# Gates and ups as pairs of 64-row half tiles, with one list of PSUM banks, in a fused attention and GeGLU kernel

## The chip, the cores and the metric

The kernel runs on one core of one Trainium2 chip. The time is device time of one execution in microseconds, the median of 3 runs: 220.92 us before (220.37 to 220.95). The profile is of one more execution, which took 221.15 us; its span, from the first to the last of the program's own instructions, is 219.4 us.

## The reference

For 2048 tokens of width 448: a layer norm, then attention over a sliding block of 256 tokens and a GeGLU feed-forward net, both on the normed x, and the sum of both with x.

```python
xn = _layernorm(x)                                     # 2048 x 448
qkv = xn @ wqkv                                        # 16 heads of 28
scores = (q @ k.T) * 28 ** -0.5                        # key within the last 256 tokens
o = softmax(scores) @ v
return x + o @ wo + (gelu(xn @ w_gate) * (xn @ w_up)) @ w_down   # F = 1792
```

## The kernel before, in words

The tokens are cut into four blocks of 512 (`qb`, 0 to 3), each of four tiles of 128. `xnT` holds the normed x transposed, 448 rows as three chunks of 128 and one of 64. The 64-row chunk stands twice, on partitions 0 to 63 and 64 to 127, so that two 64-row matmuls can use it at once, one on each half of the array's rows.

Each block has two parts. In `attention` a loop goes over steps (12 in block 0, 10 in the others): the step's score matmuls, an exponential of them on ScalarE (L622), and, at three steps, the product with the values of a group of four heads (`pv`, L576), which leaves two halves that ScalarE and VectorE add (`add_halves`). Between a step's scores and the next, TensorE is given other work from feeds: generators that issue a few matmuls and yield their cost. `gen_qk` and `gen_v` make keys, queries and values (in block 0 also those of block 1), `gen_down` makes the output of the block before (4 + 14 matmuls for each tile of tokens), and `gen_up` makes some ups early (in blocks 0 and 3), which a copy puts into `hT` (L415). A generator that yields HOLD is not run on within its step; it ends, with its 64-row matmuls, at the start of the next step. `share` and `plan` say how much of which feed goes into a step.

Then comes `gated`: for pairs of 128-wide tiles of F the gate and up products, a GELU of two tiles on ScalarE (L464), and the product of both into `hT` on VectorE (L471, or L469 for early ups). Each product is three matmuls of 128 rows (`three`, L232) and one of 64 (`half`, L238). Two 64-row matmuls on the two halves run side by side, and they are gathered: the dense matmuls of one pair, then the 64-row ones of two or three pairs, then the dense ones of the others. The last value product of the block (`last_v`) is issued behind the first 64-row ones, which in blocks 1 to 3 are cut into 32 columns, as the value product is.

The weights: `wg` and `wu` hold 384 rows of the gates and ups on 128 partitions, `wgu3` and `wug3` the last 64 rows of both, crosswise on the two halves. SyncE's queue issues nearly all loads in program order: x, the attention weights, the up weights (L144 to L146), x of tiles 8 to 11 (L147), a small part of the key weights (L174), later the DMA transposes of tiles 4 to 15 (L217), and in `loads` the gate weights and the rest. The x of tiles 0 to 3 is transposed on TensorE (`transp`).

PSUM has eight banks: four for scores or gates (`score_pool`), and four for the rest under three names: `m` (two of them), `d` and `o`. `bank` goes round a ring of names for projections and early ups, `gen_down` gets a string of names, `gated` alternates by `turn`. In blocks 1 to 3 a chunk of the output work is issued ahead of the first scores (`feeds[0].run()`).

```python
for fs in ((0, 2), (4, 8, 6), (10, 12)) if qb in (0, 3) else ((0,), (2, 4), (6, 8), (10, 12)):
    prs = [begin(fs[0])]
    dense(prs[0], True)
...
    for pr in prs:
        halves(pr, pr is not prs[0], 32 if qb and not fs[0] else P)
...
    for pr in prs[1:]:
        dense(pr, False)
        end(pr)
```

Of the kernel before, what the change touches and what calls it, by code (L numbers as in the profile page):

```python
# [75 lines left out]
def kernel(  # L76
# [38 lines left out]
    wg = const.tile([P, 3, F], bf16, name="wg")  # L115
    wu = const.tile([P, 3, F], bf16, name="wu")
    wgu3 = const.tile([P, F], bf16, name="wgu3")
    wug3 = const.tile([P, F], bf16, name="wug3")
# [3 lines left out]
    def rows(w, c0, n):  # L122
        return w[c0 * P:(c0 + n) * P, :].rearrange("(c p) n -> p c n", p=P)

# [19 lines left out]
    nc.sync.dma_start(out=wu[:, :, :], in_=rows(B_w_up, 0, 3))  # L144
    nc.sync.dma_start(out=wug3[0:64, :], in_=B_w_up[384:448, :])
    nc.sync.dma_start(out=wgu3[64:128, :], in_=B_w_up[384:448, :])  # L146
    nc.sync.dma_start(out=x_sb[:, 8:12, :], in_=xv[:, 8:12, :])  # L147
# [33 lines left out]
    xnT = const.tile([P, 4, S], bf16, name="xnT")  # L181
    qT = const.tile([P, 4, S], bf16, name="qT")
# [59 lines left out]
    ring = [("m", "m", "d"), 0]  # L242

    def bank(name):

        tag = ring[0][ring[1] % len(ring[0])]
        ring[1] += 1
        return psum.tile([P, QB], f32, name=name, tag=tag, bufs=2 if tag == "m" else 1)
# [8 lines left out]
    def v_copy(t, pv, copy):  # L257
        copy(out=v_sb[:, t, :, 0:Dh], in_=pv.rearrange("p (h d) -> p h d", d=Dh))

    def gen_v(qb, ts):  # L260

        for t in ts:
            pvs = []
            for i in range(2):
                pvs.append(bank("pv")[:, 0:D])
                v_dense(t + i, pvs[i])
                yield (570, HOLD) if i else 570
            for i in range(2):
                v_half(t + i, pvs[i])
            for i in range(2):  # L270
                v_copy(t + i, pvs[i], nc.vector.tensor_copy if qb > 1 or i else nc.scalar.copy)
            yield -360
# [10 lines left out]
    def qk_copies(qb, g, pq, pk):  # L283
        ts = slice(qb * QB, (qb + 1) * QB)
        nc.scalar.copy(out=qT[:, g, ts], in_=pq)
        nc.vector.tensor_copy(out=kT[:, g, ts], in_=pk)
        done.add((qb, g))

    def gen_qk(qb, gs, others=()):

        for g in gs:
            pq = bank("pq")[:, :]
            proj(pq, wqp, qb, g)
            if qb and g == 3:
# [4 lines left out]
                nc.scalar.copy(out=qT[:, 3, ts], in_=pq)  # L299
                done.add((qb, 3))  # L300
# [3 lines left out]
            pk = bank("pk")[:, :]  # L304
# [52 lines left out]
    UP1 = 1660  # L357
    STEP, PV = 450, 870

    hTs, oNs = {}, {}  # L360
    down_tag, last_tag, last_res = ["d"], [None], []

    def gen_down(qb, tags):

        hT, oN = hTs[qb], oNs[qb]
        for tt in range(4):
            t = 4 * qb + tt
            cs = slice(tt * P, (tt + 1) * P)
            for n, (lo, up) in enumerate(((0, D),) if t < NT - 1 else ((0, D // 2), (D // 2, D))):
                w = up - lo  # L370
                tag = tags[tt + n]
                down_tag[0] = tag
                po = psum.tile([P, QB], f32, name="po", tag=tag, bufs=2 if tag == "m" else 1)
# [11 lines left out]
                nc.vector.tensor_tensor(out=res[:, 0:w], in0=po[:, 0:w], in1=x_sb[:, t, lo:up], op=ALU.add)  # L385
                nc.sync.dma_start(out=outv[:, t, lo:up], in_=res[:, 0:w])
# [7 lines left out]
    def half(ps, f, gate, hi, ts, start, stop, m=P):  # L394

        w3 = wgu3 if gate != bool(hi) else wug3
        mm_half(ps, w3[:, f * P:(f + 1) * P], xnT[:, 3, ts], hi, start, stop, m)

    def three(ps, f, gate, ts, start, stop):
        w = wg if gate else wu  # L400
        mm3(ps, lambda c: w[:, c, f * P:(f + 1) * P], lambda c: xnT[:, c, ts], start, stop)

    def gen_up(qb, fs):

        ts = slice(qb * QB, (qb + 1) * QB)
        for f in fs:
            us = []
            for i in range(2):
                us.append(bank("ue"))
                three(us[i][:, :], f + i, False, ts, True, False)  # L410
                yield (650, HOLD) if i else 650
            for i in range(2):
                half(us[i][:, :], f + i, False, i, ts, False, True)
            for i in range(2):
                nc.vector.tensor_copy(out=hTs[qb][:, f + i, :], in_=us[i][:, :])  # L415
            yield -360

    def gated(qb, early, last_v, flush, hook):

        ts = slice(qb * QB, (qb + 1) * QB)  # L420
        hT = hTs[qb]
        turn = ["o" if down_tag[0] == "d" else "d", down_tag[0]] * 4

        def single(name, tag):
            return psum.tile([P, QB], f32, name=name, tag=tag, bufs=2 if tag == "m" else 1)[:, :]

        def begin(f, apart=False):
            last_tag[0] = turn[0] if f not in early else last_tag[0]
            pr = dict(f=f, us=[])
            if apart:  # L430
                pr["gs"] = [single("g0", tag) for tag in ("m", turn.pop(0))]
                return pr
            pr["gt"] = phase[0].pool.tile([P, 2, QB], f32, name="gt", tag="s")
            pr["gs"] = [pr["gt"][:, i, :] for i in range(2)]
            if f not in early:
                tags = ("m", turn.pop(0))
                if qb == 0 and f == 0:
                    tags = [ring[0][(ring[1] + i) % 3] for i in range(2)]
                    if "d" in tags:
                        turn.insert(0, "o")  # L440
                pr["us"] = [single("u0", tag) for tag in tags]
            return pr

        def dense(pr, start):
            f = pr["f"]
            gs = [(g, f + i, True) for i, g in enumerate(pr["gs"])]
            us = [(u, f + i, False) for i, u in enumerate(pr["us"])]
            for ps, fi, gate in (gs + us if f else us + gs):
                three(ps, fi, gate, ts, start, not start)

        def halves(pr, start, m):
            f = pr["f"]
            for i in range(2):
                if pr["us"]:
                    half(pr["gs"][i], f + i, True, 0, ts, start, not start, m)
                    half(pr["us"][i], f + i, False, 1, ts, start, not start, m)
                else:
                    half(pr["gs"][i], f + i, True, i, ts, start, not start, m)

        def end(pr):  # L460
            f = pr["f"]
            ge = work.tile([P, 2, QB], bf16, name="ge", bufs=2)
            if "gt" in pr:
                nc.scalar.activation(out=ge[:, :, :], in_=pr["gt"][:, :, :], func=ACT.Gelu_apprx_tanh)  # L464
            else:
                for i, g in enumerate(pr["gs"]):
                    nc.scalar.activation(out=ge[:, i, :], in_=g, func=ACT.Gelu_apprx_tanh)
            if not pr["us"]:
                nc.vector.tensor_tensor(out=hT[:, f:f + 2, :], in0=ge[:, :, :], in1=hT[:, f:f + 2, :], op=ALU.mult)  # L469
            for i, u in enumerate(pr["us"]):  # L470
                nc.vector.tensor_tensor(out=hT[:, f + i, :], in0=ge[:, i, :], in1=u, op=ALU.mult)  # L471
                flush()
# [478 lines left out]
```

## Time and profile before

| | |
|---|---|
| median of 3 runs | 220.92 us |
| the profiled execution, its span | 221.15 us, 219.4 us |
| first early up | 19.49 us |
| gated part of blocks 0, 1, 2, 3 begins | 37.76, 84.54, 136.03, 187.06 us |
| first scores of blocks 1, 2, 3 | 56.10, 107.58, 159.07 us |
| last output alone begins | 201.86 us |

In the views, PE is TensorE's matmuls and PEld its weight loads, DVE is VectorE, ACT ScalarE, POOL GpSimd, SP SyncE; a q behind the name is the engine's queue issuing a DMA. A timeline row gives start, length, engine, line, operation, what is written from what, the form (rows*columns of the array, then the moving operand) and how many instructions were merged. A row of the windows gives the window, its length, each engine's busy time and instructions, the granted TensorE clock, the DMA engines' share and GB/s.

### The profile page before, as it was taken

How to read it: one execution, taken by the hardware profiler on the slowest of the kernel's cores; microseconds unless marked ns; L12 is line 12 of the kernel's file. 1: busy time of each engine (PE TensorE's matmuls, PEld its weight loads, DVE VectorE, ACT ScalarE, POOL GpSimd, SP SyncE). 2: the span in 40 equal slices, each digit the busy share in tenths (PEclk: the TensorE clock that was granted, in tenths of full speed). 3: DMA queues.
4: the chain of work that ended last, by engine and by line, in shares of the span. 5: the costliest groups of instructions: out<-in, count | busy, mean ns of one | idle time of the engine just before them, and what ended most of it. 6: DMA issues, size and time to landing. Idle time of an engine off the chain costs nothing.

```text
span 219.4 us, 5447 instructions
## 1 busy us (share of the span) xinstructions
PE 213.9 (98%) x2287; PEld 96.1 (44%) x2287; DVE 152.1 (69%) x346; ACT 133.3 (61%) x131; POOL 46.9 (21%) x80
## 2 busy tenths in 40 slices
PE   7999999999999999999999999999999999999993
PEld 2433333434444454444444445444344445444562
DVE  6787896799666883679565795386356799479521
ACT  3588788662878875432878888233486777565000
POOL 5377987320000120022000022022000022022001
PEclk9999999999999999999999999999999999999998
DMA  6993799104200001102300000200000000000011
GB/s 193 310 311 71 188 325 302 30 4 72 45 3 21 24 24 27 20 3 46 60 13 24 23 1 24 52 13 0 0 3 21 25 3 24 24 1 0 22 35 37
DMA packets 18045, 13.30 MB, mean 61 GB/s; under 512 B 8704, under 2 KB 16992, under 8 KB 18016
## 3 DMA queue, kind: packets, MB, share of 16 engines
q1 hardware_dynamic: 17072, 12.62, 21.1%
q8 instruction: 19, 0.31, 0.6%
q10 hardware_dynamic: 944, 0.29, 0.5%
q14 instruction: 10, 0.08, 0.1%
HBM read 9.15 MB, written 2.18 MB: 52 GB/s over the span
## 4 chain that ended last, share of the span: by engine, by line
PE 96%; ACT 1%; DVE 1%; issue 1%; DVEq 0%
PE po L380 20%; PE gt L232 16%; PE u L232 12%; PE sc L616 6%; PE po L375 6%; PE gt L238 5%; PE ue L232 5%; PE ov L576 5%; PE pq L232 4%; PE pv L232 4%; PE pk L232 3%; PE wps L191 2%; PE pq L238 1%; PE g L232 1%; PE ue L238 1%; PE pv L238 1%
## 5 line engine op out<-in xcount | busy, mean ns | idle before, releaser
L622 ACT ACTIVATE p_sb<-sc 128x2048 bf16<-128x2048 f32 (+2 forms) x42 | 73.8, 1758 | 12.6 <-PE sc L616 8.2
L380 PE MATMUL po<-wd,hT 128*128 128x448 bf16 (+1 forms) x238 | 49.8, 342 | 0.0
L464 ACT ACTIVATE ge<-gt 128x1024 bf16<-128x1024 f32 x26 | 26.6, 1024 | 34.9 <-PE u L238 20.1
L542 POOL TENSOR_TENSOR oN<-oc,l 128x512 bf16<-128x512 f32 x12 | 16.0, 1334 | 137.8 <-DVE l L556 87.4
L232 PE MATMUL gt<-xnT,wg 128*128 128x512 bf16 x156 | 37.5, 380 | 0.0
L471 DVE TENSOR_TENSOR hT<-ge,u 128x512 bf16<-128x512 bf16 x40 | 25.7, 682 | 12.9 <-ACT ge L464 12.9
L380 PEld LDWEIGHTS <-hT 128*128 128x128 bf16 x238 | 21.5, 98 | 18.8 <-issue 2.6
L232 PE MATMUL u<-xnT,wu 128*128 128x512 bf16 x120 | 29.2, 379 | 0.0
L523 DVE TENSOR_TENSOR p_sb<-p_sb,masks 128x256 bf16<-128x256 bf16 (+1 forms) x90 | 26.8, 353 | 0.4 <-ACT p_sb L622 0.4
L232 PEld LDWEIGHTS <-wg 128*128 128x128 bf16 x168 | 15.3, 98 | 21.3 <-issue 4.5
L232 PEld LDWEIGHTS <-wu 128*128 128x128 bf16 x168 | 16.0, 98 | 19.2 <-issue 1.0
L561 DVE TENSOR_TENSOR oc<-oc,ov 128x512 f32<-128x512 f32 x12 | 8.2, 687 | 16.5 <-ACT oc L560 16.5
L616 PE MATMUL sc<-qT,kT 28*64 28x320 bf16 (+7 forms) x640 | 16.9, 263 | 0.2
L415 DVE CAST hT<-ue 128x512 bf16<-128x512 f32 x16 | 10.2, 681 | 8.4 <-PE ue L238 8.3
L375 PE MATMUL po<-wo,oN 128*128 128x448 bf16 (+1 forms) x68 | 15.9, 343 | 0.0
L385 DVE TENSOR_TENSOR res<-po,x_sb 128x448 bf16<-128x448 f32 (+1 forms) x17 | 10.0, 586 | 8.6 <-PE po L380 8.4
L533 POOL TENSOR_SCALAR_AFFINE_SELECT p_sb<-p_sb 128x512 bf16<-128x512 bf16 (+1 forms) x20 | 14.2, 730 | 5.0 <-ACT p_sb L622 4.8
L238 PE MATMUL gt<-xnT,wgu 64*128 64x512 bf16 (+1 forms) x67 | 12.7, 380 | 0.0
L560 ACT COPY oc<-ov 128x512 f32<-128x512 f32 x12 | 7.0, 583 | 8.8 <-PE ov L576 8.8
L232 PE MATMUL pq<-xnT,wqp 128*128 128x512 bf16 x45 | 12.2, 380 | 0.1
L548 DVE STREAM_TRANSPOSE l<-oc 128x512 f32<-128x512 f32 x16 | 11.3, 704 | 1.4 <-POOL oN L542 1.2
L232 PE MATMUL ue<-xnT,wu 128*128 128x512 bf16 x48 | 12.0, 380 | 0.0
(97 smaller groups left out, 241.9 us busy)
## 6 DMA issues: line engine op xcount, KB each, us to landing
out_dram<-res SPq DMA_DIRECT2D x15, 112.0 KB
x_sb<-in_A_x_dram SPq DMA_DIRECT2D x3, 448.0 KB
wu<-in_B_w_up_dram SPq DMA_DIRECT2D x1, 1344.0 KB
wg<-in_B_w_gate_dram SPq DMA_DIRECT2D x1, 1344.0 KB
wd<-in_B_w_down_dram SPq DMA_DIRECT2D x3, 448.0 KB
wraw<-in_A_wqkv_dram SPq DMA_DIRECT2D x2, 252.0 KB
wo<-in_A_wo_dram SPq DMA_DIRECT2D x4, 98.0 KB
wv<-in_A_wqkv_dram SPq DMA_DIRECT2D x1, 336.0 KB
```

The costliest lines, as they stand in the source:

```text
L232: nc.tensor.matmul(ps, lhsT=lhs(c), rhs=rhs(c), start=start and c == 0, stop=stop and c == 2, skip_group_check=True)
L238: nc.tensor.matmul(ps[c:c + m], lhsT=lhs[p0:p0 + 64, c:c + m], rhs=rhs[p0:p0 + 64], start=start, stop=stop, tile_position=(p0, c), skip_gr ...
L375: nc.tensor.matmul(po[:, 0:w], lhsT=oN[:, g, cs], rhs=wo[:, g, lo:up], start=(g == 0), stop=False, skip_group_check=True)
L380: nc.tensor.matmul(po[:, 0:w], lhsT=hT[:, f, cs], rhs=wd[:, f, lo:up], start=False, stop=(f == NF - 1), skip_group_check=True)
L464: nc.scalar.activation(out=ge[:, :, :], in_=pr["gt"][:, :, :], func=ACT.Gelu_apprx_tanh)
L471: nc.vector.tensor_tensor(out=hT[:, f + i, :], in0=ge[:, i, :], in1=u, op=ALU.mult)
L523: nc.vector.tensor_tensor(out=reg, in0=reg, in1=m, op=ALU.mult)
L533: nc.gpsimd.affine_select(out=reg, in_=reg, pattern=mid + [[1 if diag else -1, min(w, P)]], compare_op=ALU.is_ge, fill=0.0, base=0 if diag ...
L542: nc.gpsimd.tensor_tensor(out=oN[:, g, :], in0=oc[:, :], in1=inv, op=ALU.mult)
L548: nc.vector.transpose(out=l1[:, :, :].rearrange("p a b -> p (a b)"), in_=oc[:, :])
L616: nc.tensor.matmul(ss[k0:k0 + nk, j, col:col + nq], lhsT=kT[r, g, kt * P + k0:kt * P + k0 + nk], rhs=qT[r, g, qb * QB + q0:qb * QB + q0 + ...
L622: nc.scalar.activation(out=p_sb[:, :, 0:ncol], in_=ss[:, :, 0:ncol], func=ACT.Exp, scale=SCALE)
```

## The change

All 448 rows of the gate and up weights are laid out as seven chunks of 64 rows: partitions 0 to 63 hold the chunks for the first seven tiles of F, partitions 64 to 127 those for the other seven. A gate or up pair is now tile p and tile p + 7: `chunk` issues one 64-row matmul on each half, for each of seven chunks. Half of the chunks need x on the other half of the partitions, so a swapped copy of a block's x, `xsw`, is made by two DMAs (`swap`) at the start of each block. `load_ffn` loads a weight by two DMAs of 64 partitions. The up weights and x of tiles 8 to 11 are issued behind the first swap, which waits for tile 3's transposed x; the gate weights stay in `loads`.

`gated` no longer gathers: it goes from pair to pair. Early ups are pairs 1, 2, 4 in block 0 and 1 to 5 in block 3. The feed of block 0 takes the values of block 1 between the early ups, and the keys and queries of block 1 last. In block 3 a step's output work goes ahead of its early up. The chunk of output work ahead of the first scores is gone.

The four banks outside the scores are one list: `take` takes the one that is free for longest (or a named one), `give` puts it back where the last reader is issued.

```diff
-    wg = const.tile([P, 3, F], bf16, name="wg")
-    wu = const.tile([P, 3, F], bf16, name="wu")
-    wgu3 = const.tile([P, F], bf16, name="wgu3")
-    wug3 = const.tile([P, F], bf16, name="wug3")
+    wg = const.tile([P, 7, F // 2], bf16, name="wg")
+    wu = const.tile([P, 7, F // 2], bf16, name="wu")
...
+    def load_ffn(dst, w):
+        wv64 = w.rearrange("(c p) n -> p c n", p=64)
+        for hi in range(2):
+            nc.sync.dma_start(out=dst[64 * hi:64 * hi + 64, :, :], in_=wv64[:, :, hi * (F // 2):(hi + 1) * (F // 2)])
...
-    nc.sync.dma_start(out=wu[:, :, :], in_=rows(B_w_up, 0, 3))
-    nc.sync.dma_start(out=wug3[0:64, :], in_=B_w_up[384:448, :])
-    nc.sync.dma_start(out=wgu3[64:128, :], in_=B_w_up[384:448, :])
-    nc.sync.dma_start(out=x_sb[:, 8:12, :], in_=xv[:, 8:12, :])
...
+    xsw = const.tile([P, 3, QB], bf16, name="xsw")
...
-    ring = [("m", "m", "d"), 0]
+    spare = ["b0", "b1", "b2", "b3"]
+    held = {}
+
+    def take(name, cols=QB, tag=None):
+        tag = tag or spare[0]
+        spare.remove(tag)
+        ps = psum.tile([P, QB], f32, name=name, tag=tag, bufs=1)[:, 0:cols]
+        held[id(ps)] = tag, ps
+        return ps
+
+    def give(*tiles):
+        for ps in tiles:
+            spare.append(held.pop(id(ps))[0])
...
+    def swap(qb, queue):
+        ts = slice(qb * QB, (qb + 1) * QB)
+        for hi in range(2):
+            queue.dma_start(out=xsw[64 * hi:64 * hi + 64, :, :], in_=xnT[64 - 64 * hi:P - 64 * hi, 0:3, ts])
+
+    def chunk(pair, w, p, qb, c):
+        for hi, ps in enumerate(pair):
+            r = slice(64 * hi, 64 * hi + 64)
+            ts = slice(qb * QB, (qb + 1) * QB)
+            x = xnT[r, 3, ts] if c == 6 else xnT[r, c // 2, ts] if c % 2 == hi else xsw[r, c // 2, :]
+            nc.tensor.matmul(ps, lhsT=w[r, c, p * P:(p + 1) * P], rhs=x, start=c == 0, stop=c == 6,
+                             tile_position=(64 * hi, 0), skip_group_check=True)
...
+    def gen_up(qb, ps):
+        for p in ps:
+            us = [take("ue") for _ in range(2)]
+            for c in range(7):
+                chunk(us, wu, p, qb, c)
+                if c == 2:
+                    yield 640
+                if c == 5:
+                    yield 640, HOLD
...
+        up(0)
+        gate(0)
+        end(0)
+        gate(1)
+        if 1 in early:
+            end(1)
+            gate(2)
+            up(2)
+        else:
+            gate(2)
+            up(1)
+            end(1)
+            up(2)
+        end(2)
+        for p in range(3, 7):
+            gate(p)
+            up(p)
+            end(p)
...
-                if g == 2 or qb == NB - 1 and g == 3:
+                if g > 1:
                     behind.append((oc, ov))
...
-        if qb:
-            feeds[0].run()
...
-                share(feeds, want, to)
+                if qb == NB - 1:
+                    share(feeds[:1], want, 0)
+                    share(feeds, 0, to)
+                else:
+                    share(feeds, want, to)
...
     transp(3, nc.vector.tensor_copy, "b3")
+    swap(0, nc.sync)
+    load_ffn(wu, B_w_up)
+    nc.sync.dma_start(out=x_sb[:, 8:12, :], in_=xv[:, 8:12, :])
...
-            early = (2, 4, 8)
+            early = (1, 2, 4)
             feeds = [Feed((gen_qk(0, (1, 2, 3), [(t, pvs[t]) for t in (2, 3)]), 3 * QK1 + 360),
-                          (gen_up(0, (2, 8)), 2 * UP1), (gen_proj(1), PROJ), (gen_up(0, (4,)), UP1))]
+                          (gen_up(0, (1,)), UP1), (gen_v(1, (4,)), 1500), (gen_up(0, (4,)), UP1), (gen_v(1, (6,)), 1500),
+                          (gen_up(0, (2,)), UP1), (gen_qk(1, range(4)), PROJ - 3000))]
...
-                early = (2, 4, 6, 8, 10)
+                early = (1, 2, 3, 4, 5)
                 feeds.append(Feed((gen_up(3, early), UP1 * len(early))))
-                plan = {0: 1300, 2: 1300, 4: 1300, 6: 1300, 7: 1300}
+                plan = {1: 1280, 2: 1280, 4: 1280, 6: 1280, 7: 1280}
+        if qb:
+            swap(qb, nc.sync)
```

In `gated`, `gate(p)` issues the seven gate pairs into a score buffer, after the first of them the last value product, and one GELU of both tiles; `up(p)` the seven up pairs unless they were early; `end(p)` the products into `hT`.

## The prediction

> **What bounds the kernel now.** First the page: busy shares and the chain of work that ended last.
>
> ```profile
> PE 213.9 (98%) x2287; PEld 96.1 (44%) x2287; DVE 152.1 (69%) x346; ACT 133.3 (61%) x131; POOL 46.9 (21%) x80
> ...
> PE 96%; ACT 1%; DVE 1%; issue 1%; DVEq 0%
> ```
>
> TensorE ends the time nearly everywhere. The view of waits, for TensorE alone, has one row, 1.4 us in the warm-up: later no matmul stands idle for a bank, an engine or a DMA. So the time moves only by what TensorE's stream costs or by a new wait in it. A busy TensorE says nothing of how dense it is, so second the timeline of TensorE, here in the gated part of block 2:
>
> ```profile
> 143.48 1.47 PE L232 MATMUL gt<-xnT,wg 128*128 128x512 bf16 x6
> 144.79 1.46 PE L232 MATMUL u<-xnT,wu 128*128 128x512 bf16 x6
> 146.08 1.46 PE L232 MATMUL gt<-xnT,wg 128*128 128x512 bf16 x6
> 147.38 1.46 PE L232 MATMUL u<-xnT,wu 128*128 128x512 bf16 x6
> 148.77 0.39 PE L238 MATMUL gt<-xnT,wgu 64*128 64x512 bf16 x1
> ...
> 149.00 0.38 PE L238 MATMUL gt<-xnT,wgu 64*128 64x512 bf16 x1
> ...
> 149.21 0.38 PE L238 MATMUL gt<-xnT,wgu 64*128 64x512 bf16 x1
> ...
> 149.43 0.38 PE L238 MATMUL gt<-xnT,wgu 64*128 64x512 bf16 x1
> ...
> 149.74 1.47 PE L232 MATMUL gt<-xnT,wg 128*128 128x512 bf16 x6
> ```
>
> Read the starts (an end is drawn past the next start). 144.79 to 147.38 is 12 matmuls of 128 rows: 0.216 us each. Two 64-row matmuls start 3 to 10 ns apart, one on each half of the rows, and the next pair comes 0.21 to 0.23 later: a pair costs one slot. From 143.48 to 149.74 there are 24 + 4 = 28 slots, 6.04 us, but 6.26 pass. The rest, 0.22, lies at the two changes of form (147.38 to 148.77 is 1.39 for six slots, not 1.30; 149.43 to 149.74 is 0.31, not 0.22): **0.11 us for each change of the matmul's rows and columns.** The same 0.10 to 0.11 stands at the other changes of this timeline: scores (28*64), value products (64*32), dense (128*128).
>
> **Part 1, half tiles.** Gates and ups take 7 slots per two tiles before (6 dense, 1 pair) and after (7 pairs): no gain or loss in slots. What falls is changes of form. I counted them from form to form in the timeline, and again in the order that the diff writes.
>
> Block 0, from the first early up at 19.49 to the first scores of block 1 at 56.10: 36 changes. After: the three early ups lose one each (scores, 64 rows, scores); the last key/query piece, no longer beside an early up, stands alone before the gated part, +1; the gated part goes from 8 changes after its entry to 3 (half tiles, value product, half tiles, scores). 29, so 7 fewer. Blocks 1 and 2: 9 each from the entry to the next block's scores, after 4 each: 10 fewer. Part of that is the output chunk ahead of the first scores, which goes. Block 3: 6, after 4; its early ups keep 3 changes per step, since the output chunk goes first: 2 fewer. Sum 19, times 0.11: **-2.1 us**, all on the path. Bounds: 0.10 (a change without the longer second slot behind it) gives -1.9; nothing supports more than 0.11.
>
> The new weight loads (14 per two tiles, not 8) lie under the slots: the pairs at 149.00, 149.21 and 149.43 each have new weights (94 ns a load on the page by lines), and come 0.21 to 0.22 apart. If a load no longer hid, 336 new pair slots times 0.094 would cost 31.6 us.
>
> The page "TensorE: Matmul & The Clock Gate" of the Trainium skill (Part 3, what overlaps and what doesn't) says that a weight load runs beside a matmul in flight only where the row group differs. Taken alone it would make each pair wait for its loads; the spacing of the pairs above contradicts that here.
>
> **Part 2, weights behind the swapped x.** Now the loads. The third view is the timeline of all engines, the fourth the table of windows, whose last column is GB/s.
>
> ```profile
> 7.22 0.49 SPq L144 DMA_DIRECT2D wu<-in_B_w_up_dram  x1
> ...
> 9.47 0.42 DVE L228 COPY xnT<-tp 128x512 bf16<-128x512 bf16 x1 [0.54 <-PE tp L227]
> ...
> 14.54 8.37 SPq L217 DMA_TRANSPOSE xnT<-xn  x4
> ...
> 19.48 0.98 PEld L232 LDWEIGHTS <-wu 128*128 128x128 bf16 x6 [0.21 <-issue]
> ```
>
> ```profile
> 10.25:13.00 2.75, 2.75 (x22) 0.87 (x21) 2.26 (x7) 1.41 (x4) 2.32 (x11) 1.00 1.02 398
> 13.25:15.75 2.50, 2.34 (x16) 0.85 (x14) 2.33 (x7) 2.50 (x3) 1.34 (x4) 1.00 1.04 236
> ...
> 17.50:19.75 2.25, 2.18 (x18) 0.84 (x17) 2.25 (x6) 2.20 (x6) 1.84 (x4) 1.00 0.05 11
> 19.75:20.75 1.00, 1.00 (x6) 0.36 (x4) 0.36 (x1) 1.00 (x1) 1.00 (x3) 1.00 0.65 131
> ```
>
> Before, the up weights are issued at 7.22 and have slack until 19.48. In the first window the dense part (128 partitions) lands at 398 GB/s; in the second the two 64-partition remainders and the x behind them at 236 (the same pair of remainders for the gates: 222 at 26.75). After, all 1.61 MB go in two transfers of 64 partitions each, behind two swap transfers (0.39 MB) that wait for the copy ending at 9.89. A transfer shows its first bytes 1.1 us after issue (a transpose issued at 18.79; the queue is empty until 19.75). Sum: 9.9 + 1.1 = 11.0; swap at 230 GB/s 1.7, to 12.7; weights 7.0, to 19.7; from last byte to use I add 0.5 (no row of its own; bounds 0 and 1.1). Ready at 20.2, wanted at 19.49: **+0.7 us**, a new wait of TensorE. Behind it in program order stand the value product, the scores and so the exponentials: nothing fills it.
>
> Bounds: at 398 GB/s the weights take 4.0 and are ready at 17.2: no wait. The swap, SBUF to SBUF, has no row: nearest are the transposes (131 GB/s, 3.0 us, wait 2.0) and, far off, the copies of key rows from 4 partitions (47 GB/s in the window 38.5 to 41.75, 8.4 us, wait 7.4). I take 230, because the swap moves 64 partitions and whole 1 KB rows.
>
> The page "SBUF — State Buffer" of the Trainium skill (Door 1: The DMA port swizzle) speaks against this part: 64 partitions reach only 8 of 16 ports, about 218 GB/s, and two transfers to the two halves run one after the other. The trace agrees with 222 to 236. By its figure, as an estimate, the weights take 7.4 us and the wait would be about 1.2.
>
> On the same queue follow x of tiles 8 to 11 (0.46 MB at 398, to 20.9) and the transposes of tiles 4 and 5 (0.13 MB at 131, 1.0 each, to 22.9; usable 23.4). The values of tiles 4 and 5 move one step earlier: their unit starts near 22.0, tile 5's matmuls at 22.6, with the wait at 23.3: **+0.2** (0 to 0.9). The gate weights, now at half rate too, take 7.0 instead of about 5.8 us but end near 33 and are wanted near 38. The later swaps have slack: in block 3 the first early up comes some 4.6 us into the block (a full step of output work goes first) and the swap needs 1.1 + 1.7 + 0.5 after the last reader.
>
> **Part 3, one list of four banks.** TensorE waits for no bank now, so nothing can be gained. I walked the list: the tightest is the first early up, whose second bank is freed by a copy at 18.90 to 19.51; the wait for the weights covers it. A bad order would cost one copy (0.68) per block, 2.7; I take 0. Without the output chunk the next scores need the last GELU: it ends 1.27 after the last gate slot (54.33 to 55.60), and the 7 up slots last 1.51.
>
> **Sum.** -2.1 + 0.7 + 0.2 = -1.2. The profiled execution took 221.15 (span 219.4): 219.95. It lies 0.23 above the median of the runs, 220.92, so I give 219.7 for the median.
>
> **Rivals.** (a) The half-partition load is no slower, or the queue drains earlier: no wait, 220.92 - 2.1 = 218.8. For: only 128 remainder rows show the low rate, mixed with others. Against: it shows up twice. 0.18. (b) The waits just eat the gain (1.5 to 2.7 us, swap at the transposes' rate): 220.7. 0.17. (c) Slower: the swapped x goes ahead of the up weights in one queue, and SBUF to SBUF is slow. The point is a swap of 3.5 us (112 GB/s), from which wait and transposes pass 2.8 us. At 75 GB/s, between the two far rows, it takes 5.2, the weights are ready at 23.7, the wait is 4.2 + 0.2: 223.2. For: the only SBUF-to-SBUF rows are slow. Against: they move 256-byte pieces or 4 partitions. 0.14. (d) Half tiles don't do what they say, each pair paying for its loads: 252. 0.02; a small loss per pair or at banks, ending over 221.6: 0.04. The forecast itself, a wait of 0.3 to 1.4: 0.45.
>
> A difference of 0.3% (0.66 us) is about what a measurement of this kernel can tell from none. Faster: forecast and (a), 0.63. Same: (b), 0.17. Slower: (c) and (d), 0.20. The range 218.6 to 221.9 takes in (a), (b) and the bounds of the price of a change, and leaves out most of (c) and (d).
>
> **What would show it.** Steps of six dense rows and single pairs at L232/L238 give way to rows of 14 half matmuls that take 1.51 us, with 19 fewer changes of form; blocks 1 and 2, from their first gated up (84.54) to the next scores (107.58), take 0.9 us less than these 23.04: five changes, and the output chunk of 0.38 that goes elsewhere. The first early up starts near 20.2 and not at 19.49, after a wait for the DMA of the up weights, at 220 to 240 GB/s in the windows before. Wrong it would be if pairs come over 0.22 apart, if the up weights land before 19.5 or after 22, or if TensorE waits for a bank anywhere.

## The result, and the profile after

The changed kernel takes **222.94 us** in the median of six runs (222.64 to 225.15), the kernel before 220.54 in as many runs beside them (220.24 to 220.95): a ratio of 1.0124, interval 1.0082 to 1.0165. It is 1.2% slower, with the whole interval above 1, and it lies above the forecast range of 218.6 to 221.9. The profiled execution of after took 222.66 us, its span is 220.9.

The page of after, the lines of busy time and of the chain:

```profile
PE 211.8 (96%) x2572; PEld 97.4 (44%) x2581; DVE 151.9 (69%) x346; ACT 132.8 (60%) x129; POOL 47.1 (21%) x80
...
PE 92%; DMA 5%; issue 1%; DVE 1%; ACT 0%; DVEq 0%
```

TensorE is busy for 2.1 us less, and the chain holds 5% of DMA where before it held none that the line showed. The view of TensorE's waits says which DMAs:

```profile
PE ue L424 <- DMA wu<-in_B_w_up_dram: 2.1, 1, 2.1
PE wps L194 <- DVE wo L170: 1.4, 1, 1.4
PE pv L235 <- DMA xnT<-xn: 1.3, 1, 1.3
```

The middle row is the warm-up's, as before. The other two are new, one wait each. The timeline of TensorE has both (the bracket is the idle time ahead of the row):

```profile
19.53 0.39 PE L424 MATMUL ue<-xnT,wu 64*128 64x512 bf16 x1
22.02 0.39 PE L424 MATMUL ue<-xsw,wu 64*128 64x512 bf16 x2 [2.11 <-DMA wu<-in_B_w_up_dram]
...
24.24 0.34 PE L624 MATMUL sc<-qT,kT 28*128 28x384 bf16 x4
25.90 1.31 PE L235 MATMUL pv<-wv,xnT 128*128 128x448 bf16 x6 [1.32 <-DMA xnT<-xn]
```

The first early up begins at 19.53 with one half, whose weights came in the first of the two transfers, and then stands until 22.02 for the second. The loss there is the whole 2.49 between the two starts, since a half that runs alone saves nothing of the pair's slots; the wait's row counts only the 2.11 behind the first half's drawn end. Later the values of tiles 4 and 5 stand until 25.90 for the transposes: the four scores ahead of them take 0.28 (as at 21.81 before), so 1.38 are lost.

Now the gain, again TensorE's timeline of after, in the gated part of block 0:

```profile
49.80 0.38 PE L424 MATMUL u<-xnT,wu 64*128 64x512 bf16 x1
...
51.31 0.38 PE L424 MATMUL gt<-xnT,wg 64*128 64x512 bf16 x1
```

From one product to the next, seven pairs take 1.51 us, 0.216 each, each with new weights. Counted from form to form over the whole of TensorE's stream, the changes of form went from 161 to 142: 19 fewer, as forecast. Stage by stage, from the first early up (19.49 before, 19.53 after) and from the first matmuls of each stage in the timelines; the last column is an experiment of below:

| us | before | after | weights apart and early |
|---|---|---|---|
| attention of block 0, from the first early up | 18.27 | **21.99** | 18.66 |
| gated 0 | 18.34 | 17.44 | 17.44 |
| attention 1 | 28.44 | 28.86 | 28.99 |
| gated 1 | 23.04 | 22.03 | 22.04 |
| attention 2 | 28.45 | 28.86 | 28.85 |
| gated 2 | 23.04 | 22.03 | 22.03 |
| attention 3 | 27.99 | 28.36 | 28.37 |
| gated 3 | 14.80 | 14.49 | 14.48 |
| last output, to the end | 17.57 | 17.35 | 17.43 |
| sum | 199.94 | 201.41 | 198.29 |

Each attention of blocks 1 to 3 gets the output chunk (0.38) that stood ahead of its first scores, and each gated part loses that and its changes of form. Taken with that, gated 0 to gated 3 and attention 1 to 3 are 2.03 us shorter. All of the loss, 3.72, is in one stage. Counting from the first early up leaves out the run-up, which differs between profiles by itself: the same code reaches that point at 19.49 us in before and at 18.98 in `b_singles` below.

### The profile page after: what moved, and what is told of

Its sections match the earlier page's. It is cut to its first block, busy times and chain, and to the rows that moved or that the text cites. A ratio compares the mean times of both kernels' runs of the same rounds, so it can differ in the third digit from the quotient of the medians.

```text
span 220.9 us, 6047 instructions
## 1 busy us (share of the span) xinstructions
PE 211.8 (96%) x2572; PEld 97.4 (44%) x2581; DVE 151.9 (69%) x346; ACT 132.8 (60%) x129; POOL 47.1 (21%) x80
## 4 chain that ended last, share of the span: by engine, by line
PE 92%; DMA 5%; issue 1%; DVE 1%; ACT 0%; DVEq 0%
PE po L395 20%; PE gt L424 19%; PE u L424 14%; PE po L390 6%; PE sc L624 6%; PE ue L424 5%; DMA xnT<-xn 5%; PE ov L585 4%; PE pv L235 4%; PE pq L235 4%; PE pk L235 3%; PE wps L194 2%; PE pq L241 1%; PE pv L241 1%; PE s L235 1%
## 5 line engine op out<-in xcount | busy, mean ns | idle before, releaser
L465 ACT ACTIVATE ge<-gt 128x1024 bf16<-128x1024 f32 x28 | 28.7, 1023 | 39.5 <-PE gt L424 38.9
L424 PE MATMUL gt<-xnT,wg 64*128 64x512 bf16 x224 | 45.3, 376 | 0.0
L424 PE MATMUL gt<-xsw,wg 64*128 64x512 bf16 x168 | 40.7, 376 | 0.0
L424 PE MATMUL u<-xnT,wu 64*128 64x512 bf16 x160 | 33.2, 376 | 0.0
L424 PEld LDWEIGHTS <-wu 64*128 64x128 bf16 x392 | 18.7, 94 | 26.2 <-issue 3.8
L395 PEld LDWEIGHTS <-hT 128*128 128x128 bf16 x238 | 21.4, 98 | 18.7 <-issue 2.8
L424 PE MATMUL u<-xsw,wu 64*128 64x512 bf16 x120 | 29.1, 376 | 0.0
L424 PEld LDWEIGHTS <-wg 64*128 64x128 bf16 x392 | 18.8, 94 | 22.7 <-issue 0.3
L424 PE MATMUL ue<-xnT,wu 64*128 64x512 bf16 x64 | 13.6, 377 | 0.0
L424 PE MATMUL ue<-xsw,wu 64*128 64x512 bf16 x48 | 11.3, 378 | 2.1 <-DMA wu<-in_B_w_up_dram 2.1
L624 PEld LDWEIGHTS <-kT 28*64 28x64 bf16 (+1 forms) x640 | 7.7, 102 | 11.4 <-issue 9.9
```

What stands on the lines that cost most here:

```text
L395: nc.tensor.matmul(po[:, 0:w], lhsT=hT[:, f, cs], rhs=wd[:, f, lo:up], start=False, stop=(f == NF - 1), skip_group_check=True)
L424: nc.tensor.matmul(ps, lhsT=w[r, c, p * P:(p + 1) * P], rhs=x, start=c == 0, stop=c == 6, tile_position=(64 * hi, 0), skip_group_check=True)
L465: nc.scalar.activation(out=ges[p][:, :, :], in_=gt[:, :, :], func=ACT.Gelu_apprx_tanh)
L624: nc.tensor.matmul(ss[k0:k0 + nk, j, col:col + nq], lhsT=kT[r, g, kt * P + k0:kt * P + k0 + nk], rhs=qT[r, g, qb * QB + q0:qb * QB + q0 + ...
```

## The experiments

The theory after the result: the two waits are the whole loss, and they come of the rate at which 64 partitions take data, not of the swap ahead of the weights and not of the half tiles. Rivals: the place alone (late in the queue behind the swap), the swap's own speed, and a cost of the half tiles or of the new order in `gated`.

### The weights late, on 128 partitions and on 64

Two kernels that keep the kernel before, half tiles and all else left out, and only load the up weights where the changed kernel does, behind a swap of block 0's x. That swap goes into an unused part of `wg`, and nothing reads it. In `b_late_full` the dense part stays on 128 partitions:

```diff
-    nc.sync.dma_start(out=wu[:, :, :], in_=rows(B_w_up, 0, 3))
-    nc.sync.dma_start(out=wug3[0:64, :], in_=B_w_up[384:448, :])
-    nc.sync.dma_start(out=wgu3[64:128, :], in_=B_w_up[384:448, :])
-    nc.sync.dma_start(out=x_sb[:, 8:12, :], in_=xv[:, 8:12, :])
...
     transp(3, nc.vector.tensor_copy, "d")
+    for hi in range(2):
+        nc.sync.dma_start(out=wg[64 * hi:64 * hi + 64, :, 0:QB], in_=xnT[64 - 64 * hi:P - 64 * hi, 0:3, 0:QB])
+    nc.sync.dma_start(out=wu[:, :, :], in_=rows(B_w_up, 0, 3))
...
```

> The kernel before, with the up weights moved behind a swap transfer of block 0's x (into a part of the gate weights that is loaded later; nothing reads it) but still loaded on 128 partitions. My theory (the loss is the half-partition load, not its late place): swap done at 13.0, weights at about 400 GB/s usable near 18.5, no wait at the first early up (19.5 us); time as before within 0.3 us. Rival (the late place alone is enough): TensorE waits over 1 us for the up weights, +1 to +2 us.

In `b_late_half` only the dense part's transfer is cut in two:

```diff
-    nc.sync.dma_start(out=wu[:, :, :], in_=rows(B_w_up, 0, 3))
+    for a in range(2):
+        nc.sync.dma_start(out=wu[64 * a:64 * a + 64, :, :], in_=rows(B_w_up, 0, 3)[64 * a:64 * a + 64])
```

> As the run with the late load, but with the dense up weights in two transfers of 64 partitions each. My theory: about 215 GB/s, weights usable near 22, a wait of about 2.3 us at the first early up; the transposes behind it are wanted a step later here and cost 0 to 0.5: +2 to +3 us against before. Rival (the place counts, not the partitions): the same time as the run that loads 128 partitions.

The windows from 13 to 18 us, first of `b_late_full`, then of `b_late_half` (last column GB/s):

```profile
13.00:18.00 5.00, 4.79 (x29) 1.76 (x31) 4.78 (x14) 4.57 (x5) 3.67 (x8) 1.00 1.00 331
```

```profile
13.00:18.00 5.00, 4.79 (x29) 1.76 (x30) 4.78 (x14) 4.58 (x5) 3.67 (x8) 1.00 0.98 221
```

Same bytes, same place, same work beside them: 331 against 221 GB/s. In `b_late_full` no matmul waits for a DMA and the first early up stands at 19.53, as before. In `b_late_half` it waits, and the second early up comes 1.72 us later than before (23.81, not 22.09). The row shows 1.24 of it, at the dense part (20.77 for 19.53); nearly all of the rest comes at the 64-row remainders loaded behind it, where the second of the two matmuls starts at 22.61 and the first at 22.16:

```profile
20.77 1.46 PE L228 MATMUL ue<-xnT,wu 128*128 128x512 bf16 x6 [1.18 <-DMA wu<-in_B_w_up_dram]
```

Times: 221.27 (1.0036, 1.0017 to 1.0055) and 222.91 (1.0091, 1.0073 to 1.011). So the place behind the swap makes no wait by itself; cutting one transfer into two halves of the partitions makes one. The wait is shorter than the 2.3 that I expected at the first early up; the time, 2.1 over the kernel before, is within the 2 to 3 expected. That `b_late_full` is 0.36% slower its profile does not show (span 219.6, before 219.4; every stage within 0.05): the profiled execution of before, 221.15, lies itself above the 220.79 of the runs beside this one. It stays open.

### The kernel before with more changes of form

The price of a change was read from gaps. Here the kernel before is made to have 28 more of them: the 64-row matmuls are no longer gathered, each pair ends with its own.

```diff
-        for fs in ((0, 2), (4, 8, 6), (10, 12)) if qb in (0, 3) else ((0,), (2, 4), (6, 8), (10, 12)):
+        for fs in ((0,), (2,), (4,), (8,), (6,), (10,), (12,)) if qb in (0, 3) else ((0,), (2,), (4,), (6,), (8,), (10,), (12,)):
```

> The kernel before, with the 64-row matmuls of the gated parts no longer gathered: each pair has its own. The work and the slots are the same, the changes of form are 28 more (8, 6, 6, 8 in the four blocks). My theory (each change costs 0.105 us on the path): +2.9 us. Rival (the changes are drawn in the trace but partly hidden, so the half tiles gained less than 2 us): under +1.5 us.

226.91, ratio 1.0276 (1.026 to 1.0293). The profiled execution, 226.03, is the fastest of the five. Its span is 224.3, 4.9 longer than before's, and from the first early up to the end it is 5.4 longer, since its run-up happens to be 0.5 shorter. The waits of TensorE have a row that explains much of what is above the 2.9 expected, and the timeline shows one of the three:

```profile
PE sc L616 <- ACT ge L464: 2.0, 3, 0.7
```

```profile
161.95 0.55 PE L375 MATMUL po<-wo,oN 128*128 128x448 bf16 x2
163.17 0.42 PE L616 MATMUL sc<-qT,kT 28*64 28x320 bf16 x16 [0.67 <-ACT ge L464]
```

Three times the next block's scores wait for the last GELU, since the last 64-row matmuls of the gate now come at the very end. From the output chunk to the scores it is 1.22 where it was 0.47 before (107.11 to 107.58), so each wait costs 0.75 and the three 2.3. That leaves 3.1 for 28 changes, 0.11 each. The price of Part 1 holds; the total that I expected left out this wait. The median lies 6.1 above the kernel before, and the 0.7 or so that the profile does not have isn't explained.

### The queue behind the weights

`a_x_late` is the changed kernel with x of tiles 8 to 11 loaded in `loads`, so that the transposes of tiles 4 and 5 stand right behind the weights.

```diff
     load_ffn(wu, B_w_up)
-    nc.sync.dma_start(out=x_sb[:, 8:12, :], in_=xv[:, 8:12, :])
...
+        nc.sync.dma_start(out=x_sb[:, 8:12, :], in_=xv[:, 8:12, :])
         nc.sync.dma_start(out=x_sb[:, 12:16, :], in_=xv[:, 12:16, :])
```

> The changed kernel, with x of tiles 8 to 11 taken from behind the up weights and put with the later loads, behind the transposes. My theory (the second wait, 1.3 us, is the transposes of tiles 4 and 5 queued behind 0.46 MB of x): that wait falls to 0 to 0.3, -1.0 to -1.3 us against the changed kernel; the wait for the up weights stays 2.1 to 2.3. Rival (the transposes are slow by themselves when they start that late): the wait stays over 1 us, no gain.

221.79 (1.0045, 1.0024 to 1.0066): 1.0 above the kernel before beside it, where after was 2.4 above. Of the two waits one row is left:

```profile
PE ue L424 <- DMA wu<-in_B_w_up_dram: 2.0, 1, 2.0
```

The wait for the weights stays and that for the transposes is gone. The second wait was the queue's: 0.46 MB of x between the weights and the transposes.

### The weights early, the swap last, and two queues

`a_wu_early` puts the up weights (and x of tiles 8 to 11) back where they were before, and leaves the swap behind them, all in one queue.

```diff
+    load_ffn(wu, B_w_up)
+    nc.sync.dma_start(out=x_sb[:, 8:12, :], in_=xv[:, 8:12, :])
...
     swap(0, nc.sync)
-    load_ffn(wu, B_w_up)
-    nc.sync.dma_start(out=x_sb[:, 8:12, :], in_=xv[:, 8:12, :])
```

> The changed kernel, with the up weights and x of tiles 8 to 11 issued where they were before, so that the swap comes last in the queue. My theory (half-rate load, one queue in order): weights from about 9.9 to 17.4, x to 18.6, swap to 20.4 and usable near 21: the first early up waits 1.0 to 1.8 us, now for the swapped x; the transposes come behind the swap, near 22.5, and cost 0 to 0.8. About 1 to 2 us under the changed kernel. Rival (the waits have nothing to do with the order of the queue): no gain.

```profile
PE ue L426 <- DMA xsw<-xnT: 2.0, 1, 2.0
```

223.93 (1.0122, 1.008 to 1.0163): no better than after; the 1 to 2 us that I expected did not come. The wait has its old length and another name. Whatever stands last among weights, x and swap is used at 21.4 to 22.0 us. The profiled execution took 222.28 at a mean clock of 0.992; what makes four others take 223.9 to 224.4, at 0.990 to 0.992, isn't shown, and the clock does not tell them apart.

`a_wu_early_swap_act` is the same with the first swap issued on ScalarE's queue.

```diff
-    swap(0, nc.sync)
+    swap(0, nc.scalar)
```

> As the run with the early up weights, but the first swap is issued by ScalarE's queue, beside the weights and not behind them. My theory: swap done near 14, weights usable near 19 to 20, a wait of 0 to 0.5 us, transposes near 21.5: the 19 fewer changes of form show nearly whole, 2 us under the kernel before (0.988 to 0.993 of it). Rival (half tiles gain nothing, the lost time is elsewhere): the time of the kernel before or more.

220.85 (1.003, 1.0002 to 1.0057), not the 0.988 to 0.993 that I expected: TensorE waits 1.2 for the swap and 0.4 for the transposes. The swap is issued from 9.22 on, but by the packets, which the trace lists with start and size (a row of the swap is 1024 bytes, one of the weights 1792), it moves only from 15.92 to 19.61, while the weights move from 9.09 to 18.84. A queue of its own did not let it pass: the two queues moved 238 GB/s between them (8 to 17 us).

`a_two_queues` is the changed kernel with the second half of the up weights on ScalarE's queue.

```diff
-            nc.sync.dma_start(out=dst[64 * hi:64 * hi + 64, :, :], in_=wv64[:, :, hi * (F // 2):(hi + 1) * (F // 2)])
+            queues[hi].dma_start(out=dst[64 * hi:64 * hi + 64, :, :], in_=wv64[:, :, hi * (F // 2):(hi + 1) * (F // 2)])
...
-    load_ffn(wu, B_w_up)
+    load_ffn(wu, B_w_up, (nc.sync, nc.scalar))
```

> The changed kernel, with the second half of the up weights issued by ScalarE's queue, in the same place. If two transfers to the two halves of the partitions run together at the full rate once they are in two queues: weights usable near 18 to 19, no first wait, and the second falls too: 2 to 3.5 us under the changed kernel. If they share one rate of about 215 GB/s whatever the queue: usable near 22, the time of the changed kernel within 0.5 us.

221.78 (1.0045, 1.0011 to 1.0078), the middle of two groups: six executions at 220.1 to 220.9 with a mean clock of 0.998 or more, the profiled one among them, and six at 222.6 to 224.9 with 0.984 to 0.992. The second half moves from 9.5 us on, ahead of the swap, since ScalarE's queue does not wait for tile 3. The wait falls to 1.1 and that for the transposes goes, while the values of a tile now wait 0.4 for a bank (for the copy of an early up, by the view of waits); the rate from 14 to 20 us is 235 GB/s. But the second half ends at 14.19 and the first starts at 14.79, so the two did not move at once: of the two cases that I had set out this run decides neither.

`a_halves_apart` asks that alone: x of tiles 8 to 11 late, and both the swap and the up weights as two transfers on two queues, partitions 0 to 63 on one, 64 to 127 on the other.

```diff
-    swap(0, nc.sync)
-    load_ffn(wu, B_w_up)
-    nc.sync.dma_start(out=x_sb[:, 8:12, :], in_=xv[:, 8:12, :])
+    swap(0, nc.sync, nc.scalar)
+    load_ffn(wu, B_w_up, (nc.sync, nc.scalar))
```

> The changed kernel with x of tiles 8 to 11 late, and the two halves of the first swap and of the up weights in two queues: SyncE issues those for partitions 0 to 63, ScalarE those for 64 to 127, so that both halves are in flight at once. If each half of the partitions has its own rate of about 215 GB/s, the weights move at about 400 GB/s and are usable near 17 to 18: no wait, 218.5 to 219 us (2 us under the kernel before). If one rate of about 215 GB/s holds for whatever moves in pieces of 64 partitions: usable near 21 to 22, a wait of 1.5 to 2.3, 221 to 222 us.

The window over the swap and the weights:

```profile
12.00:20.00 8.00, 7.38 (x53) 2.75 (x51) 7.35 (x20) 7.44 (x11) 5.72 (x13) 1.00 1.05 230
```

230 GB/s for two transfers to the two halves, the rate of one; it is 229 from 14.5 to 17.5, where packets of weights from both queues move side by side. A theory that two queues would bring some 400 falls. The time is 220.62 (1.0022, 1.0 to 1.0045), 0.4 under the 221 to 222 that I expected for one rate, with a wait of 1.1 for the weights. Beside `a_x_late`, which differs from it by the second queue alone, the weights move in 7.6 us and not 8.0, and TensorE happens to want them 0.5 later. The page "SBUF — State Buffer" of the Trainium skill (section "Can I just issue two DMAs to hit both halves?") says the same: transfers to the two halves gain almost nothing over one, from whichever engine they are issued. This run agrees.

### Enough time for the bytes

If the rate is fixed, only an earlier start helps. In `a_early_apart` half of the up weights go where they were before, half on ScalarE's queue behind one of its copies (issued at 8.15), the swap follows on SyncE's queue, and x of tiles 8 to 11 is late.

```diff
+    load_ffn(wu, B_w_up, his=(0,))
...
     pads(nc.scalar.copy, wkp, slice(0, 1))
+    load_ffn(wu, B_w_up, (None, nc.scalar), his=(1,))
...
-    swap(0, nc.sync)
-    load_ffn(wu, B_w_up)
-    nc.sync.dma_start(out=x_sb[:, 8:12, :], in_=xv[:, 8:12, :])
+    swap(0, nc.sync, nc.sync)
```

> The changed kernel with x of tiles 8 to 11 late, the up weights for partitions 0 to 63 issued by SyncE where the up weights were before, those for 64 to 127 by ScalarE behind its copy of key weights at about 9.4 us, and the first swap by SyncE. By the theory that the waits for DMAs are all that cost time: weights usable near 16 to 19, swap before 19, no wait over 0.3, 218.4 to 219.2 us. Rival (something else in the changed kernel costs 1 us or more): 220 us or over without a wait for a DMA in the trace.

**219.28 us** (219.11 to 219.92), ratio 0.9947 (0.9931 to 0.9962): 0.5% faster than the kernel before, with the whole interval below 1. TensorE's waits are the warm-up row alone, at the same rate, started earlier:

```profile
PE wps L195 <- DVE wo L171: 1.4, 1, 1.4
```

```profile
10.00:18.00 8.00, 7.84 (x52) 2.80 (x50) 7.27 (x21) 6.29 (x11) 6.24 (x18) 1.00 1.08 222
```

Outside block 0's attention the change is now what Part 1 said. Its column in the table is 1.65 us under before; what it lacks to 2.1 lies in block 0's attention. (The medians differ by 1.15 only. The column leaves out what comes ahead of the first early up, and the 0.5 between the two isn't explained.) There TensorE's timeline shows two small steps that the view of waits does not list:

```profile
19.18 0.39 PE L425 MATMUL ue<-xnT,wu 64*128 64x512 bf16 x1
19.66 0.39 PE L425 MATMUL ue<-xsw,wu 64*128 64x512 bf16 x2
...
28.34 0.39 PE L425 MATMUL ue<-xnT,wu 64*128 64x512 bf16 x1
28.46 0.49 PE L425 MATMUL ue<-xsw,wu 64*128 64x512 bf16 x2
```

The second half of a pair should start with the first. At 19.66 it comes 0.48 later, and the early up ends that much later: from 19.18 to the value products at 21.26 it takes 2.08, not seven slots and a change, 1.62. Two things end shortly before: the copy that frees its bank (VectorE, 18.60 to 19.21) and the swap, whose last packet ends at 18.88. No run separates them, but the lags speak for the swap. Where the view of waits names a DMA for the first early up, the matmul starts 0.7 to 1.0 behind that transfer's last packet (0.88 in after, 1.00 in `a_x_late`); here it is 0.78. The 0.12 at 28.46 has its swap long behind it and fits the bank: it is 0.05 behind the end of a copy of values by ScalarE (27.88 to 28.41), as the same step in after is (32.14, copy to 32.09). The matmul at 19.66 is 0.45 behind its copy.

### The stretch behind the wait

The executions of `a_x_late` fall into two groups: four at 221.05 to 221.4 with a mean granted clock of 0.998 to 0.999, and five with 0.990 to 0.992, four of them at 222.3 to 222.7 and one at 221.79. Its profiled execution is of the upper group. The windows and TensorE's timeline behind the wait:

```profile
22.00:25.30 3.30, 3.30 (x31) 0.98 (x27) 1.29 (x2) 0.00 (x0) 2.18 (x11) 0.50 0.80 186
```

```profile
21.45 0.39 PE L424 MATMUL ue<-xsw,wu 64*128 64x512 bf16 x2 [2.05 <-DMA wu<-in_B_w_up_dram]
...
24.12 1.15 PE L585 MATMUL ov<-p_sb,v_sb 128*32 128x128 bf16 x16
25.20 0.38 PE L624 MATMUL sc<-qT,kT 28*128 28x384 bf16 x4
```

The granted clock is 0.50 (third column from the end), and the sixteen value products take 1.08 us to the next row, where they take 0.60 in the kernel before (21.21 to 21.81). So an idle stretch of 2 us is followed by 3.4 us at half clock, in some executions; in the profiled execution of after, 2.1 us were followed by none. To test it, the wait was filled: nine 64-row matmuls ahead of the first early up, whose sum is overwritten.

The first try, `a_x_late_fill`, is void. Its filler read the warm-up's zeros, into whose place `wo` is loaded, so that TensorE stood 18.0 us for that load (242.16). It tells nothing on this question.

> The changed kernel with x of tiles 8 to 11 late, and nine 64-row matmuls on zeros ahead of the first early up, into a bank that is written anew afterwards: 1.95 us, where TensorE waits 2.0 for the up weights. Theory (the wait itself costs its length, and in some executions TensorE's clock falls to half for 3.4 us behind it, another 1.7 us): executions near 222.5 with a granted clock of 0.99 vanish, all lie at 220.9 to 221.6. Rival (the spread comes from the DMAs): as many executions over 222 as without the filling (5 of 9).

`a_x_late_fill2` reads the value weights and x instead:

```diff
             us = [take("ue") for _ in range(2)]
+            for _ in range(9 if (qb, p) == (0, 1) else 0):
+                nc.tensor.matmul(us[0], lhsT=wv[0:64, 0, 0:P], rhs=xnT[0:64, 0, 0:QB], start=True, stop=True,
+                                 tile_position=(0, 0), skip_group_check=True)
```

> The kernel with x of tiles 8 to 11 loaded late, and TensorE's wait of 2.0 us for the up weights filled with nine 64-row matmuls of data that is there (9 x 0.216 = 1.95 us; their sum is overwritten, so that nothing of the output changes). The filler saves no time by itself: a free wait would be replaced by work. Theory that the lost executions (222.3 to 222.7 at a mean clock of 0.99, beside 221.1 to 221.4 at 0.998) come of TensorE's idle stretch: with the stretch filled none is left near 222.5, all lie at 220.9 to 221.6 with a mean clock of 0.997 or more, and no window behind 20 us shows 0.5. Rival, that they come of something else of this order of loads: as many executions above 222 as without the filler (5 of 9 before). A second way to fall: the nine matmuls come late as well and the wait stays, then it tells nothing.

Beside it on the same chip ran `a_x_late` once more, unchanged:

> The kernel with x of tiles 8 to 11 loaded late, as it was, on the same chip as the filled one: the two peaks again, some half of its executions near 222.5 at a mean clock of 0.99 and the others near 221.2 at 0.998. If all lie at one of the two, the comparison with the filled kernel on this chip says only so much.

With the filler all 12 executions have a mean clock of 0.997 or more and take 220.57 to 221.86 (median 221.24; 1.0028, 1.0015 to 1.004). Without it three of 8 have 0.989 to 0.991 and take 222.15 to 222.36, and five have 0.996 or more and take 221.12 to 221.58 (median 221.49; 1.0042, 1.0025 to 1.0059). The windows behind the stretch, first of the filled kernel, then of the other, whose profiled execution is one of the three:

```profile
22.00:23.00 1.00, 1.00 (x10) 0.46 (x12) 0.00 (x0) 0.00 (x0) 1.00 (x2) 1.00 2.65 59
```

```profile
22.00:23.00 1.00, 1.00 (x8) 0.32 (x5) 0.00 (x0) 0.00 (x0) 1.00 (x5) 0.50 0.39 69
```

The spread is wider than I expected (220.9 to 221.6), but the upper group is gone. Useless work in place of the idle stretch keeps the clock up. It is worth some 0.8 us in those executions, and it cannot win back the wait itself.

## Why the prediction was wrong, point by point

The forecast for the median was 219.7, and 222.94 came. Between the profiled executions, which the sum was made for, it was 219.95 and 222.66: a miss of 2.71. Two terms of Part 2 failed, the wait for the up weights (0.7 forecast, 2.49 measured) and the wait for the transposes behind them (0.2 forecast, 1.38 measured). Both were new waits as foretold, and both were sized too small, because the load of the weights on 64 partitions ended later than its bytes divided by 230 GB/s; the transposes added 1.1 us of their own.

| step | forecast | measured in after |
|---|---|---|
| changes of form outside block 0's attention (17) | -1.9 | -2.03 |
| wait for the up weights | +0.7 | +2.49 |
| wait for the transposes of tiles 4 and 5 | +0.2 | +1.38 |
| block 0's attention beside the waits (2 changes) | -0.2 | -0.15 |
| first early up, last output and tail | 0 | -0.2 |
| sum | -1.2 | +1.5 |

**Part 1 was right**: 19 changes fewer, 0.11 to 0.12 us each (2.03 for the 17 outside block 0's attention, 3.1 for the 28 of `b_singles`), and the new weight loads cost nothing. Blocks 1 and 2 went from 23.04 to 22.03, a little more than the 0.9 foretold.

**Part 2 failed in its sizes; the mechanism was as described.** The swap moved its bytes from 11.25 to 13.0 (forecast 11.0 to 12.7), so 230 GB/s was a fair value for it. The weights then took 8.2 us, not 7.0. The windows of after, over the swap, the start of the weights, their middle and their end:

```profile
11.25:13.00 1.75, 1.75 (x17) 0.54 (x17) 1.33 (x4) 1.41 (x4) 1.46 (x7) 1.00 0.90 224
13.00:14.00 1.00, 0.95 (x4) 0.40 (x6) 1.00 (x5) 0.91 (x1) 0.86 (x4) 1.00 0.77 108
14.00:20.00 6.00, 5.69 (x39) 1.97 (x37) 5.76 (x15) 5.61 (x9) 4.37 (x8) 1.00 1.07 234
20.00:21.25 1.25, 0.00 (x0) 0.00 (x0) 0.15 (x1) 1.25 (x1) 0.98 (x2) 1.00 1.08 214
```

The first microsecond runs at 108 GB/s, but the next at 305 (206 over both), so it is not the start that costs. By the trace's packets the weights move from 12.94 to 21.14: 1.61 MB in 8.2 us, 196 GB/s. 99% of the packets have begun by 20.49, 7.6 us in, at 210 GB/s; the last few need 0.65 more, and x of tiles 8 to 11 already moves beside them (most of the 214 in the last window is x). So the rate was 210 and not 230, and my division of bytes by rate had no term for a thin end; each is worth about 0.6. The last packet ends at 21.14 and the matmul starts at 22.02, 0.9 later, where I had added 0.5. Start 0.2 late, 1.2 more of transfer, 0.4 more to use: ready at 22.0, not 20.2, at the edge of what I had named as wrong. The bound for a slower load was missing too: only the swap's rate had one, the weights' rate had none on the slow side.

The page "SBUF — State Buffer" of the Trainium skill (Door 1) has a second figure beside the 218 that the prediction cited: 196 GB/s measured for a 1 MiB transfer to 64 partitions. The measured average, over two transfers of 0.80 MB one behind the other, is the same number. By the 218 I had estimated a wait of about 1.2, half of the measured one.

The transposes inherited that delay. They stood in the queue behind x of tiles 8 to 11, whose end I had put at 20.9 and which came at 22.3, and then they came in bursts. The windows of after:

```profile
22.00:23.25 1.25, 1.23 (x12) 0.60 (x13) 0.00 (x0) 0.00 (x0) 1.25 (x3) 1.00 2.67 221
23.25:24.50 1.25, 1.25 (x25) 0.38 (x20) 0.96 (x2) 0.00 (x0) 1.25 (x10) 1.00 0.13 6
```

Between two bursts only 6 GB/s move for 1.25 us; why they pause isn't shown. Usable was 25.9, not 23.4: 1.4 of that is the delay ahead of the transposes (22.3 for 20.9), 1.1 their own pace. `a_x_late` confirms the queue as the cause.

**Part 3** took 0 for the bank list, and in after nothing of block 0's attention is left over beside the waits, so the cover that I named held. Without it a price shows: in `a_early_apart` that stage is 0.39 longer than before, where two changes fewer make it 0.2 shorter. The 0.6 are the late second halves at 19.66 (0.48, by its lag the swap) and 28.46 (0.12, by its lag a bank). In `a_two_queues` the values of a tile wait 0.4 for a bank outright. So the list cost 0.1 to 0.4 us in these two profiles; no run tried the half tiles without it.

**Not foreseen at all** was the clock behind a wait. In after it matters little: its profiled execution has a clock of 1.000 and took 222.66; the others have 0.985 to 0.992 and took 222.64 to 223.57, one 225.15. My reading of the equal times is that a TensorE at half clock needs the transposes later, and so uses up the second wait; no execution of after with the lower clock was traced.

**The rivals.** The number came out near rival (c), 223.2, by luck and by another road. Its point was a swap of 3.5 us; the swap took 1.75 and decided nothing. It named the right place (the weights behind the swap in one queue, the transposes behind both) and the wrong transfer. No rival had the weights themselves as the slow ones, although the rate of 64 partitions stood in the same paragraph. (a) is out by `b_late_half`, (d) by the pairs at 0.216.

The median of before was 220.54 in these runs, and its profiled execution, 221.15, 0.6 above it; that of after lies 0.3 below its median. So the profiles differ by 1.5 us and the medians by 2.4.

## What to carry to other kernels

A layout that puts a tensor on half of the partitions pays for it in its load: 1.61 MB took 8.2 us where 128 partitions took data at 331 to 398 GB/s, and a second queue did little (7.6 us for 8.0); only an earlier start took the wait away. When a load is moved, forecast its end with three terms, the rate of the bulk, the thin end (0.65 us here) and the time from the last packet to use (0.7 to 1.0), bound each on both sides, and do the same for everything behind it in the queue. A saving of 0.11 us per change of form is real and adds up, but it needs the loads to have slack: with them early the same change won 0.53%.

## What the runs showed of the hardware

- **A wait of 2 us can halve the clock behind it.** `a_x_late` stood 1.7 to 2.0 us and then ran 3.4 us at a granted clock of 0.50, in eight of its 17 executions by their mean clock; filled, in none of 12. After stood 2.1 us without it in its profiled execution, so it is not every time. In `a_x_late_fill` the clock fell some 4.4 us into the stand of 18.0 us and came back 7 us after its end. The page "TensorE: Matmul & The Clock Gate" of the Trainium skill (Part 1) has the clock fall after an idle window of some 3.4 us and come back after a busy one as long, with the windows running on by themselves. The length of the half-clock stretch in `a_x_late` agrees; the idle time that sufficed here was shorter.
- **Two transfers to the two halves share one rate**, 229 GB/s from two queues in `a_halves_apart`, 234 from one in after (14 to 20 us). A swap on a queue of its own still moved 5 us after it was issued, behind most of the weights (`a_wu_early_swap_act`). Cutting a 128-partition transfer in two took the rate from 331 to 221.
- **A swap from SBUF to SBUF** of 64 partitions in rows of 1 KB moves at 224 GB/s, as fast as a load from memory to as many partitions.
- **Pairs of 64-row matmuls sustain 0.216 us with new weights for each**, 14 weight loads of 94 ns in 1.51 us.
- **From the last packet of a load to the matmul that waits for it** 0.7 to 1.0 us pass, in the seven runs in which the first early up of the changed kernel waits for weights or a swap.
